# Spectral mixing and gated FFN: splitting the spectrum straight from its bank, mixing in two steps, and three smaller edits

## The chip, the cores and the metric

The kernel runs on one core of one Trainium2 chip. The metric is device time in microseconds (us), the median of several runs. Five engines work side by side, each through its own queue of instructions in order: PE (TensorE, matmuls; PEld is its weight load), DVE (VectorE), ACT (ScalarE), POOL (GpSimd) and SP (SyncE, which here only issues DMAs). An instruction whose inputs aren't ready holds up everything behind it on its engine.

## What is computed

```python
def _attn_ref(x, w_r, w_i, b_r, b_i):           # x: 8 x 3008 x 256
    X = np.fft.rfft(x, axis=1)
    Xr, Xi = X.real, X.imag
    Yr = Xr @ w_r - Xi @ w_i + b_r
    Yi = Xr @ w_i + Xi @ w_r + b_i
    Yr = np.sign(Yr) * np.maximum(np.abs(Yr) - 0.01, 0.0)   # Yi likewise
    return np.fft.irfft(Yr + 1j * Yi, n=x.shape[1], axis=1)

def _moe_ref(x, w_gate, w_val, w_out):          # x: 24064 x 256, hidden 1536
    g = x @ w_gate
    return (g / (1 + np.exp(-g)) * (x @ w_val)) @ w_out
```

A Fourier transform along the sequence, a complex 256x256 mix of the channels, a soft threshold, the inverse transform, and then a gated feed-forward network over all 24064 tokens.

## The kernel before, in words

**Two parts.** `transform` does the spectral part for 8 batches; `gated_ffn` does the feed-forward network for 24 blocks of tokens. The FFN's instructions are put in order by hand. In the transform a scheduler decides at build time in which order each engine runs its instructions, from the order in which the program emits them and from what depends on what.

**The transform.** The length 3008 is factored as 47 x 64. For each batch:

- `stage_a` (16 chunks `ch`): a load of the tokens, one fp32 matmul by the 47-point matrix into bank `ps_a` (L295, two hardware matmuls in the trace), a copy to SBUF by ACT (L298), and a store to a DRAM buffer `d1` (L299). Batch 0 goes first and alone: its loads (L286) are issued at once, its matmuls use four banks in turn, and its copies go to the tile tags "a", "z", "t" in turn, two buffers each.
- `stage_b` (12 pairs `p` of frequencies): a load `a_in` (L306), four fp32 matmuls into the one bank `ps_b` (L311), a copy `f` by ACT (L315), the sum of real and imaginary part by POOL (L316), and the split of all three (real, imaginary, sum: 768 columns) into two parts for the mix: `f_hi`, rounded to float32r (L318, DVE), and `f_lo`, what is left over (L319, DVE). `f`, `f_hi` and `f_lo` have two buffers each.
- `stage_mix`: six matmuls of the sum with one weight into bank `ps_s` (L329), an add of the bias by DVE that spreads the result over a bank `mixb0` or `mixb1` (L331), twelve matmuls onto that bank (L337), four copies that regroup it into `t` (L349, ACT), the soft threshold (L350 on DVE, L351 on POOL) and the split of the result into `y_hi` (L354, ACT) and `y_lo` (L355, DVE).
- `stage_bi`: three matmuls into `ps_z` (L368; six for a batch's first pair, L365), a copy `z` (L370, ACT) and a store to a buffer `d2` (L371).
- `stage_ai` (8 units): a load `z_in` (L379), matmuls into two banks `ps_x` (L388), copies `xt` (L395, ACT) and a store to `xt_d` (L396), from which the FFN reads its tokens.

All of this is emitted slot by slot: 96 slots, one for each (batch, pair). In slot `s` stand `stage_bi` of pair s-2, `stage_mix` of pair s-1 and `stage_b` of pair s; the `stage_a` and `stage_ai` of other batches and the preparation of the FFN's weights (L213 to L257: DVE, POOL and ACT) are spread over the slots by a few rates. Slots from 98 on are emitted by `finish`.

**The FFN's start.** `load_x(0)` loads the first block's tokens; `x_sum` makes four sums of it (L502, POOL); `x_part` splits seven operands into a float32r part (L510, ACT) and what is left (L511, POOL). The first matmul of the FFN is L745; L516 is the helper through which all its products go, three matmuls each. The first pass over a unit of weights uses the operands in the order 1, 5, 6, 2, 7, 3, 4.

Of the kernel before, what the change touches and what calls it, by code (L numbers as in the profile page):

```python
# [18 lines left out]
B = 8  # L19
# [94 lines left out]
def f32(ap):  # L114
    return ap.bitcast(F32)
# [30 lines left out]
def transform(ctx, tc, front, last, ps_, xp, w_r, w_i, cb, wup_raw, wdn_raw, ca, cf, ci, co, wdn, wup_d, xt_d, d2):  # L146
# [143 lines left out]
    def stage_a(b, ch, xt):  # L290
        if ch == 0:
            d1[b] = dram.tile([NK, P, C], F32, name="d1", tag="d1")
        tag = "absz"[ch % 4] if b == 0 else "a"
        ps = ps_.tile([P, T], F32, name="ps_a", tag="ps_" + tag)
        nc.tensor.matmul(ps[:96], lhsT=wa, rhs=xt, start=True, stop=True)  # L295
        tag = "azt"[ch % 3] if b == 0 else "a"
        a = sb.tile([96, T], F32, name="a", tag=tag)
        nc.scalar.copy(a, ps[:96])  # L298
        store = nc.sync.dma_start(d1[b].rearrange("k (q m) c -> (k q) (m c)", m=NM)[:, ch * T : (ch + 1) * T], a)  # L299
        if b == 0 and ch == NCH - 1:  # L300
            gates.append(store)


    def stage_b(b, p):
# [3 lines left out]
        for cc in range(2):  # L308
            for k in range(2):
                s = (cc * 2 + k) * P  # L310
                nc.tensor.matmul(ps[:, s : s + P], lhsT=t[:, k, cc * P : (cc + 1) * P], rhs=wf[:, 2 * p + k, :], start=True, stop=True)  # L311
        f = sb.tile([P, 3 * C], F32, name="f", tag="f", bufs=2)
        hi = sb.tile([P, 3, 2, P], F32R, name="f_hi", tag="f_hi")
        lo = sb.tile([P, 3, 2, P], F32R, name="f_lo", tag="f_lo")
        nc.scalar.copy(f[:, : 2 * C].rearrange("p (q a b) -> p a q b", q=2, b=64), ps.rearrange("p (a q b) -> p a q b", q=2, b=64))  # L315
        nc.gpsimd.tensor_tensor(f[:, 2 * C :], f[:, :C], f[:, C : 2 * C], op=ALU.add)  # L316
        flat = lambda x: x.rearrange("p q a b -> p (q a b)")
        v.tensor_copy(flat(hi), f)  # L318
        v.tensor_tensor(flat(lo), f, f32(flat(hi)), op=ALU.subtract)  # L319
        return hi, lo  # L320

    def stage_mix(b, p, parts):

# [3 lines left out]
        for cc in range(2):  # L327
# [83 lines left out]
    for b in range(B):  # L411
        base = NP * b
        for p in range(NP):
            s = base + p
            at(s, lambda b=b, p=p: fs.__setitem__((b, p), stage_b(b, p)))
            at(s + 1, lambda b=b, p=p: ys.__setitem__((b, p), stage_mix(b, p, fs.pop((b, p)))))
            at(s + 2, lambda b=b, p=p: stage_bi(b, p, ys.pop((b, p))))
    for k in range((B - 1) * NCH):
# [28 lines left out]
    for s in sorted(slots):  # L447
        if s < B * NP + 2:
            for fn in slots[s]:
                fn()  # L450
        gates += stores
        stores.clear()

    def finish():
        for s in sorted(slots):
            if s >= B * NP + 2:
                for fn in slots[s]:
                    fn()
# [4 lines left out]
def gated_ffn(ctx, tc, front, ring, ps_, co, wdn, wup_d, xt_d, d2, out):  # L463
# [35 lines left out]

    def x_sum(blk, o, a, b):  # L500
        f = lambda i: raws[blk][:, i, :]
        g.tensor_tensor(f(o), f(a), f(b), op=ALU.subtract)  # L502

    SUMS = ((4, 0, 1), (6, 2, 4), (5, 2, 0), (7, 3, 6))

    def x_part(blk, n_):
        h = BLOCKS[blk][1]
        src = raws[blk][:, X_AT[n_], :]
        part = xs[blk][n_] = sb.tile([P, 2, T], F32R, name="x_parts", bufs=12)
        act.copy(part[:, 0, :h], src)  # L510
        g.tensor_tensor(part[:, 1, :h], src, f32(part[:, 0, :h]), op=ALU.subtract)  # L511

# [306 lines left out]
```

## Time and profile before

| | us |
|---|---|
| median of 3 runs | 2745.8 (2737.93 to 2747.36) |
| the profiled execution's own time | 2740.56 |
| its span in the profile | 2738.8 |
| PE busy in the span | 2655.4 |
| DVE, POOL, ACT busy | 2087.3, 2061.7, 1712.2 |
| first matmul of the FFN starts | 679.88 |

The granted TensorE clock of the profiled execution is 0.991 of full speed on the mean. A row of the timeline gives start, duration, engine, line, operation, output and input, the count of merged instructions, and in square brackets the idle time before it and what ended that. Ends of matmuls are modelled, so a busy PE isn't PE at its peak.

### The profile page before, as it was taken

To read this page: it belongs to the slowest core of one execution; us is meant where nothing else is said; L and a number is where in the kernel's file an instruction comes from. 1 tells how busy PE (TensorE), PEld (TensorE's weight loads), DVE (VectorE), ACT (ScalarE), POOL (GpSimd) and SP (SyncE) were. 2 spreads that over 40 slices of the span, in tenths; PEclk is the share of its full clock that TensorE was granted. 3 is DMA by queue.
4 is the path that set the end of the run, shared out by engine and by line. 5 is a ranking of instruction groups with operands and counts; after the bars stand their busy time and mean duration, and the time that the engine had idled before them with its cause. 6 is when DMAs were issued, how large, how long until landed. Compare 5 with 4: busy or idle time off the path is not lost. (4 is left out here: it accounts for less than half of the span.)

```text
span 2738.8 us, 39634 instructions
## 1 busy us (share of the span) xinstructions
PE 2655.4 (97%) x13173; PEld 2207.0 (81%) x13173; DVE 2087.3 (76%) x2916; ACT 1712.2 (63%) x3280; POOL 2061.7 (75%) x1574
## 2 busy tenths in 40 slices
PE   8989998989999999999999999999999999999998
PEld 5777787778788888888888888888888888888898
DVE  3776677775778777887787877787778877888787
ACT  4666666666566666666666666666665666666665
POOL 1454465564888888888888888888888888888885
PEclk9999999999999999999999999999999999999999
DMA  8889898766354444444454444444454444444453
GB/s 251 256 271 294 283 293 267 229 197 203 137 172 156 156 141 164 168 155 157 140 171 161 150 156 149 170 156 157 140 172 156 162 144 146 154 164 153 146 185 105
DMA packets 180124, 491.88 MB, mean 180 GB/s; under 512 B 17264, under 2 KB 89584, under 8 KB 179824
## 3 DMA queue, kind: packets, MB, share of 16 engines
q1 hardware_dynamic: 179920, 489.35, 54.0%
q8 instruction: 105, 1.72, 0.3%
q14 instruction: 99, 0.81, 0.1%
HBM read 378.65 MB, written 110.62 MB: 179 GB/s over the span
## 5 line engine op out<-in xcount | busy, mean ns | idle before, releaser
L516 PE MATMUL bank<-x_parts,wup 128*128 128x512 f32 (+1 forms) x6048 | 1518.2, 386 | 1.2 <-POOL x_parts L511 0.7
L516 PEld LDWEIGHTS bank<-x_parts,wup 128*128 128x128 f32 x6048 | 1125.8, 188 | 226.5 <-DVE bank L645 5.4
L536 POOL TENSOR_TENSOR h_parts<-more,h_parts 128x512 fp32r<-128x512 f32 (+1 forms) x573 | 847.6, 1492 | 113.9 <-ACT h_parts L532 99.8
L536 POOL TENSOR_TENSOR h_parts<-hidden,h_parts 128x512 fp32r<-128x512 f32 (+1 forms) x432 | 565.1, 1316 | 204.0 <-ACT h_parts L532 164.5
L516 PE MATMUL bank<-h_parts,wdn_hi 128*128 128x512 f32 (+1 forms) x2016 | 613.5, 385 | 0.9 <-POOL h_parts L536 0.9
L532 ACT CAST h_parts<-hidden 128x512 fp32r<-128x512 f32 (+1 forms) x432 | 265.0, 613 | 451.3 <-DVE hidden L618 451.3
L516 PEld LDWEIGHTS bank<-h_parts,wdn_hi 128*128 128x128 f32 x2016 | 378.2, 188 | 74.1 <-POOL h_parts L536 1.8
L618 DVE TENSOR_TENSOR hidden<-hidden,bank 128x512 f32<-128x512 f32 (+1 forms) x576 | 376.0, 674 | 77.6 <-PE bank L516 69.2
L557 DVE TENSOR_TENSOR sums<-sums,bank 128x512 f32<-128x512 f32 (+1 forms) x360 | 241.9, 672 | 245.1 <-PE bank L516 245.1
L516 PE MATMUL bank<-h_parts,wdn_lo 128*128 128x512 f32 (+1 forms) x1008 | 388.6, 386 | 4.2 <-DVE sums L557 4.2
L532 ACT CAST h_parts<-more 128x512 fp32r<-128x512 f32 (+1 forms) x576 | 351.4, 610 | 41.8 <-DVE more L527 31.3
L616 ACT ACTIVATE hidden<-bank 128x512 f32<-128x512 f32 (+1 forms) x432 | 252.2, 584 | 117.6 <-PE bank L516 117.2
L527 DVE TENSOR_TENSOR more<-hidden 128x512 f32<-128x512 f32 (+1 forms) x288 | 293.0, 1056 | 0.0
L527 DVE TENSOR_TENSOR more<-hidden,more 128x512 f32<-128x512 f32 (+1 forms) x288 | 258.6, 898 | 0.0
L351 POOL TENSOR_TENSOR t<-t,y 128x512 f32<-128x512 f32 x96 | 133.4, 1389 | 136.6 <-DVE y L350 136.6
L645 DVE TENSOR_TENSOR bank<-hidden,bank 128x512 f32<-128x512 f32 (+1 forms) x288 | 197.0, 684 | 45.0 <-PE bank L516 32.2
L623 ACT COPY bank<-bank 128x512 f32<-128x512 f32 (+1 forms) x288 | 161.6, 561 | 109.4 <-DVE hidden L618 104.0
L516 PEld LDWEIGHTS bank<-h_parts,wdn_lo 128*128 128x128 f32 x1008 | 189.5, 188 | 40.8 <-issue 4.5
L511 POOL TENSOR_TENSOR x_parts<-xf,x_parts 128x512 fp32r<-128x512 f32 (+1 forms) x168 | 209.9, 1268 | 11.5 <-PE bank L516 7.1
L316 POOL TENSOR_TENSOR f<-f 128x256 f32<-128x256 f32 x96 | 85.3, 889 | 146.0 <-ACT f L315 142.9
L631 ACT COPY hidden<-bank 128x512 f32<-128x512 f32 (+1 forms) x288 | 167.6, 582 | 2.6
L349 ACT COPY t<-mixb 64x256 f32<-64x256 f32 x384 | 140.6, 366 | 29.6 <-PE mixb L337 20.1
(94 smaller groups left out, 3273.3 us busy)
## 6 DMA issues: line engine op xcount, KB each, us to landing
wup<-wup_d SPq DMA_DIRECT2D x288, 896.0 KB, 4.6
d<-a SPq DMA_DIRECT2D x128, 192.0 KB, 4.2
a_in<-d SPq DMA_DIRECT2D x96, 256.0 KB, 4.5
out<-o SPq DMA_DIRECT2D x88, 256.0 KB, 6.1
scratch<-xp SPq DMA_DIRECT2D x116, 192.0 KB, 4.6
d<-z SPq DMA_DIRECT2D x84, 256.0 KB, 3.8
z_in<-d SPq DMA_DIRECT2D x56, 384.0 KB, 5.1
xt_d<-xt SPq DMA_DIRECT2D x56, 376.0 KB, 4.4
```

Of the source, the lines that this page charges most:

```text
L349: nc.scalar.copy(t[64 * half : 64 * half + 64, k * C : (k + 1) * C], mixb[64 * k : 64 * k + 64, half * C : (half + 1) * C])
L511: g.tensor_tensor(part[:, 1, :h], src, f32(part[:, 0, :h]), op=ALU.subtract)
L516: nc.tensor.matmul(o, lhsT=weights[w], rhs=parts[x], start=start and i == 0, stop=stop and i == 2, skip_group_check=True)
L527: v.tensor_tensor(at(o, h), at(a, h), at(b, h), op=ALU.subtract)
L532: act.copy(pair[i][:, 0, :h], at(i, h))
L536: eng.tensor_tensor(pair[i][:, 1, :h], at(i, h), f32(pair[i][:, 0, :h]), op=ALU.subtract)
L557: v.tensor_tensor(o, o, spare[:, :h], op=ALU.add)
L616: act.activation(at(i, h), src, AF.Silu)
L618: v.tensor_tensor(at(i, h), at(i, h), src, op=ALU.mult)
L623: act.copy(b3[:, :h], b1[:, :h])
L631: act.copy(m5, b2[:, :h])
L645: v.tensor_tensor(b2[:, :h], m5, b3[:, :h], op=ALU.add)
```

## The change

Four edits.

1. **Batch 0's copies** go in turn to six tags instead of three, "a", "z", "t", "y", "y_hi", "y_lo": twelve buffers instead of six.
2. **The split in `stage_b`** is taken from the bank `ps_b` itself. ACT writes `f_hi` of the real and the imaginary part from the bank (512 columns, L320 of the changed kernel) and copies the real part to `f` (256 columns, L321). DVE adds the imaginary part from the bank (L322) and takes `f_lo` of both parts, bank minus `f_hi` (L323). The sum's own split is ACT's for the upper part (L324) and DVE's for the lower (L325). POOL has no work left here. `f_hi` and `f_lo` get three buffers each; `f` is a third of its size.
3. **The mix in two steps.** The six matmuls and the bias add become `stage_sum`, one slot after `stage_b`; the rest stays `stage_mix`, one slot later; `stage_bi` comes one slot later than it did. `finish` begins at slot 99.
4. **The FFN's first block.** The split of operand 1 is emitted ahead of the sums; the four sums go to DVE; of the seven lower parts those of operands 6, 7 and 4 go to DVE, and 1, 5, 2 and 3 stay on POOL. Later blocks are as before.

```diff
-        tag = "azt"[ch % 3] if b == 0 else "a"
+        tag = ("a", "z", "t", "y", "y_hi", "y_lo")[ch % 6] if b == 0 else "a"
         a = sb.tile([96, T], F32, name="a", tag=tag)
...
-        f = sb.tile([P, 3 * C], F32, name="f", tag="f", bufs=2)
-        hi = sb.tile([P, 3, 2, P], F32R, name="f_hi", tag="f_hi")
-        lo = sb.tile([P, 3, 2, P], F32R, name="f_lo", tag="f_lo")
-        nc.scalar.copy(f[:, : 2 * C].rearrange("p (q a b) -> p a q b", q=2, b=64), ps.rearrange("p (a q b) -> p a q b", q=2, b=64))
-        nc.gpsimd.tensor_tensor(f[:, 2 * C :], f[:, :C], f[:, C : 2 * C], op=ALU.add)
-        flat = lambda x: x.rearrange("p q a b -> p (q a b)")
-        v.tensor_copy(flat(hi), f)
-        v.tensor_tensor(flat(lo), f, f32(flat(hi)), op=ALU.subtract)
+        total = sb.tile([P, 2 * P], F32, name="f", tag="f", bufs=2)
+        hi = sb.tile([P, 3, 2, P], F32R, name="f_hi", tag="f_hi", bufs=3)
+        lo = sb.tile([P, 3, 2, P], F32R, name="f_lo", tag="f_lo", bufs=3)
+        both = ps.rearrange("p (a q b) -> p a q b", q=2, b=64)
+        first = lambda x: x[:, :2].rearrange("p q c (k b) -> p (c k) q b", b=64)
+        blocks = lambda x: x.rearrange("p (a b) -> p a b", b=64)
+        flat = lambda x: x[:, 2].rearrange("p c a -> p (c a)")
+        nc.scalar.copy(first(hi), both)
+        nc.scalar.copy(blocks(total), both[:, :, 0])
+        v.tensor_tensor(blocks(total), blocks(total), both[:, :, 1], op=ALU.add)
+        v.tensor_tensor(first(lo), both, f32(first(hi)), op=ALU.subtract)
+        nc.scalar.copy(flat(hi), total)
+        v.tensor_tensor(flat(lo), total, f32(flat(hi)), op=ALU.subtract)
         return hi, lo
 
-    def stage_mix(b, p, parts):
+    def stage_sum(b, p, parts):
...
+        return parts
+
+    def stage_mix(b, p, parts):
+
+        mixb = mixed[p % 2]
         for half, (q, i) in enumerate(((1, 2), (0, 1))):
...
-            at(s + 1, lambda b=b, p=p: ys.__setitem__((b, p), stage_mix(b, p, fs.pop((b, p)))))
-            at(s + 2, lambda b=b, p=p: stage_bi(b, p, ys.pop((b, p))))
+            at(s + 1, lambda b=b, p=p: fs.__setitem__((b, p), stage_sum(b, p, fs.pop((b, p)))))
+            at(s + 2, lambda b=b, p=p: ys.__setitem__((b, p), stage_mix(b, p, fs.pop((b, p)))))
+            at(s + 3, lambda b=b, p=p: stage_bi(b, p, ys.pop((b, p))))
...
-    for sums_ in SUMS:
-        x_sum(0, *sums_)
-    for n_ in X_AT:
-        x_part(0, n_)
+    x_part(0, 1)
+    for sums_ in SUMS:
+        x_sum(0, *sums_, eng=v)
+    for n_ in list(X_AT)[1:]:
+        x_part(0, n_, v if n_ in (6, 7, 4) else g)
```

**What moves on the engines.** The rows below are the built program's order on one engine; a name with a number, like ps_x_7095 or mixb_120, is one buffer or bank of that name.

ACT, one of the last slots of the transform, before:

```order
L349 COPY t<-mixb_120 64x256 x4
L315 COPY f<-ps_b 128x4x2x64
L395 COPY xt<-ps_x_7095 128x376
L395 COPY xt<-ps_x_7101 128x376
L370 COPY z<-ps_z 128x512
L354 CAST y_hi<-t 128x512
```

The same place in the changed program (L360 is the old L349, L406 the old L395, L381 the old L370, L365 the old L354):

```order
L320 CAST f_hi<-ps_b 128x4x2x64
L321 COPY f<-ps_b 128x256
L360 COPY t<-mixb_120 64x256 x4
L324 CAST f_hi<-f 128x256
L406 COPY xt<-ps_x_7268 128x376
L381 COPY z<-ps_z 128x512
L406 COPY xt<-ps_x_7274 128x376
L365 CAST y_hi<-t 128x512
```

One ACT instruction on a pair's spectrum has become three, and the four copies of `t` now stand between the second and the third.

DVE, one slot near the end of the transform, before:

```order
L318 CAST f_hi<-f 128x768
L355 TENSOR_TENSOR y_lo<-t,y_hi 128x512
L319 TENSOR_TENSOR f_lo<-f,f_hi 128x768
L331 TENSOR_TENSOR mixb_121<-ps_s,bias 128x512
L350 TENSOR_SCALAR y<-t 128x512
```

The same engine in the changed program (L366 is the old L355, L337 the old L331, L361 the old L350):

```order
L366 TENSOR_TENSOR y_lo<-t,y_hi 128x512
L322 TENSOR_TENSOR f<-f,ps_b 128x256
L323 TENSOR_TENSOR f_lo<-ps_b,f_hi 128x4x2x64
L337 TENSOR_TENSOR mixb_121<-ps_s,bias 128x512
L361 TENSOR_SCALAR y<-t 128x512
L325 TENSOR_TENSOR f_lo<-f,f_hi 128x256
```

The two wide instructions of the split have become three narrower ones, two of which read the bank.

PE, the end of the transform and the FFN's first matmul, before (here the number behind a name is one tile; ps_z_7276 is the last pair's):

```order
L337 MATMUL mixb1_121<-wm1_lo_116,f_hi_7171 128x256
L368 MATMUL ps_z_7209<-y_hi_7159,wi_hi_111 128x512
L368 MATMUL ps_z_7209<-y_lo_7160,wi_hi_111 128x512
L368 MATMUL ps_z_7209<-y_hi_7159,wi_lo_112 128x512
L368 MATMUL ps_z_7276<-y_hi_7244,wi_hi_111 128x512
L368 MATMUL ps_z_7276<-y_lo_7245,wi_hi_111 128x512
L368 MATMUL ps_z_7276<-y_hi_7244,wi_lo_112 128x512
L745 MATMUL bank_7293<-x_parts_7314,wdn_hi_60 128x512
```

The same place in the changed program (L348 is the old L337, L379 the old L368, L399 the old L388, L759 the old L745; ps_z_7468 is the last pair's):

```order
L348 MATMUL mixb1_121<-wm1_lo_116,f_hi_7330 128x256
L379 MATMUL ps_z_7437<-y_hi_7397,wi_hi_111 128x512
L399 MATMUL ps_x0_7424<-wo_956,z_in_7368 128x94 x4
L379 MATMUL ps_z_7437<-y_lo_7398,wi_hi_111 128x512
L379 MATMUL ps_z_7437<-y_hi_7397,wi_lo_112 128x512
L399 MATMUL ps_x1_7430<-wo_956,z_in_7368 128x94 x4
L379 MATMUL ps_z_7468<-y_hi_7464,wi_hi_111 128x512
L379 MATMUL ps_z_7468<-y_lo_7465,wi_hi_111 128x512
L379 MATMUL ps_z_7468<-y_hi_7464,wi_lo_112 128x512
L759 MATMUL bank_7485<-x_parts_7502,wdn_hi_60 128x512
```

Eight matmuls of the last `stage_ai` have moved from earlier on PE to between the last mix and the last `ps_z`.

More of the change, by code (lines that the diff above doesn't have):

```diff
@@ L447, in transform @@
     for s in sorted(slots):
-        if s < B * NP + 2:
+        if s < B * NP + 3:
             for fn in slots[s]:
@@ L455, in finish @@
         for s in sorted(slots):
-            if s >= B * NP + 2:
+            if s >= B * NP + 3:
                 for fn in slots[s]:
@@ L498, in load_x, with x_sum, x_part @@
         xs[blk] = {}
-    def x_sum(blk, o, a, b):
+    def x_sum(blk, o, a, b, eng=g):
         f = lambda i: raws[blk][:, i, :]
-        g.tensor_tensor(f(o), f(a), f(b), op=ALU.subtract)
+        eng.tensor_tensor(f(o), f(a), f(b), op=ALU.subtract)
     SUMS = ((4, 0, 1), (6, 2, 4), (5, 2, 0), (7, 3, 6))
-    def x_part(blk, n_):
+    def x_part(blk, n_, eng=g):
         h = BLOCKS[blk][1]
@@ L510, in x_part @@
         act.copy(part[:, 0, :h], src)
-        g.tensor_tensor(part[:, 1, :h], src, f32(part[:, 0, :h]), op=ALU.subtract)
+        eng.tensor_tensor(part[:, 1, :h], src, f32(part[:, 0, :h]), op=ALU.subtract)
     def product(o, weights, parts, start, stop):
```

## The prediction

> **What bounds the kernel now.** I read the windows of the whole span first: each engine's busy time, then the granted TensorE clock and the DMA share.
>
> ```profile
> 0.00:40.00 40.00, 27.10 (x65) 12.98 (x65) 6.08 (x11) 14.30 (x25) 1.45 (x6) 0.87 0.86 244
> 40.00:240.00 200.00, 184.68 (x1164) 148.44 (x1164) 136.49 (x195) 131.12 (x284) 99.21 (x92) 0.98 0.84 265
> 240.00:440.00 200.00, 183.93 (x1223) 153.05 (x1222) 145.10 (x198) 130.26 (x285) 109.26 (x99) 0.98 0.88 291
> 440.00:640.00 200.00, 177.73 (x1256) 155.55 (x1255) 148.66 (x201) 127.52 (x282) 118.29 (x102) 0.98 0.73 228
> 640.00:680.00 40.00, 35.72 (x273) 33.03 (x271) 18.72 (x31) 27.94 (x63) 11.46 (x12) 0.96 0.55 179
> 690.00:2738.80 2048.80, 2037.14 (x9176) 1698.69 (x9174) 1630.91 (x2281) 1274.80 (x2331) 1713.41 (x1258) 1.00 0.46 155
> ```
>
> From 690 us on PE is busy 2037.14 of 2048.80 us: the FFN is bound by PE, and the change leaves it alone but for its first block. All that can move lies ahead of 690. From 40 to 640 PE is busy 184.68 + 183.93 + 177.73 = 546.3 of 600 us and idle 53.7; in the first 40 us it is idle 12.9. No other engine is full there: DVE 430.2, ACT 388.9, POOL 326.8 of 600. So the transform is bound by PE plus the waits of PE, and the waits of PE between 40 and 640 us tell what a change of the other engines can be worth:
>
> ```profile
> PE mixb L337 <- DVE mixb L331: 18.7, 22, 2.1
> PE ps_x L388 <- DMA z_in<-d: 9.4, 10, 2.1
> PE ps_z L368 <- DVE y_lo L355: 8.7, 9, 3.0
> PE ps_a L295 <- ACT a L298: 6.0, 7, 3.1
> PE ps_z L368 <- ACT y_hi L354: 4.1, 5, 1.6
> PE ps_z L368 <- ACT z L370: 3.7, 4, 2.2
> ```
>
> The columns are us in total, times, and the longest. The largest is the bias add L331 coming late; y_lo and y_hi (12.8) end the soft threshold's chain over ACT, DVE and POOL.
>
> **Edit 1, twelve buffers.** Batch 0's matmuls on PE, and the copy on ACT that held them up:
>
> ```profile
> 18.83 2.52 ACT L298 COPY a<-ps_a 96x512 f32<-96x512 f32 x5 [4.77 <-DMA d<-a]
> 9.76 7.11 PE L295 MATMUL ps_a<-x_first,wa 96*96 96x512 f32 x16 [0.82 <-DMA x_first<-xp]
> 19.46 5.37 PE L295 MATMUL ps_a<-x_first,wa 96*96 96x512 f32 x8 [2.59 <-ACT a L298]
> 24.67 1.88 PE L295 MATMUL ps_a<-scratch,wa 96*96 96x512 f32 x4
> 15.00:20.00 5.00, 2.41 (x7) 0.76 (x6) 0.00 (x0) 1.17 (x3) 0.00 (x0) 1.00 0.95 312
> 20.00:25.00 5.00, 5.00 (x9) 1.74 (x8) 0.00 (x0) 2.65 (x6) 0.00 (x0) 0.66 0.80 259
> 25.00:30.00 5.00, 1.55 (x4) 0.33 (x2) 0.00 (x0) 1.61 (x3) 0.00 (x0) 1.00 0.67 200
> ```
>
> The seventh copy waited 4.77 us for the first store to land; PE stood 2.59 us and then ran its next eight matmuls at 0.67 us each instead of 7.11 / 16 = 0.44, the granted clock at 0.66. With twelve buffers copies 7 to 12 need no store, and the first store has landed before the thirteenth. The last twelve matmuls would take 12 x 0.44 = 5.3 us from 16.87, ending at 22.2 instead of 26.55: 4.4 us. But the DMA engines were idle only 0.05 + 0.20 + 0.33 of 5 us each there, 2.9 us, and the same bytes must pass. Bounds 1 (earlier stores delay the last loads) and 4.4; I take **3.5**.
>
> The Trainium skill, "TensorE: Matmul & The Clock Gate", section "What's actually happening", has the clock halve only after an idle window of about 3.4 us; here the granted clock is down after a gap of 2.59 us. By that page the drop needn't go with the gap, and this edit would give the gap alone, 2.6, and the sum below would be 0.9 smaller.
>
> **Edits 2 and 3, the steady slots.** The groups of the split and the mix, 40 to 640 us:
>
> ```profile
> L315 ACT COPY f<-ps_b 128x512 f32<-128x512 f32 x92 | 54.0, 587 | 59.0 <-DVE f_lo L319 51.2 <-PE ps_b L311 4.0 <-PE ps_x L388 1.6
> L316 POOL TENSOR_TENSOR f<-f 128x256 f32<-128x256 f32 x92 | 82.4, 896 | 103.0 <-ACT f L315 99.9 <-DVE y L350 3.0
> L318 DVE CAST f_hi<-f 128x768 fp32r<-128x768 f32 x90 | 73.1, 813 | 46.4 <-PE mixb L337 43.7 <-POOL f L316 2.7
> L319 DVE TENSOR_TENSOR f_lo<-f,f_hi 128x768 fp32r<-128x768 f32 x91 | 102.7, 1128 | 1.4
> L331 DVE TENSOR_TENSOR mixb<-ps_s,bias 128x512 f32<-128x512 f32 x90 | 62.1, 690 | 0.5 <-PE ps_s L329 0.5
> L349 ACT COPY t<-mixb 64x256 f32<-64x256 f32 x356 | 130.4, 366 | 27.7 <-PE mixb L337 18.5 <-ACT z L370 2.0 <-issue 2.0
> L354 ACT CAST y_hi<-t 128x512 fp32r<-128x512 f32 x88 | 54.6, 620 | 57.4 <-POOL t L351 56.9
> ```
>
> The new widths by the nearest rows:
>
> ```profile
> 34.10 0.40 ACT L210 CAST wi_hi<-raw_i 128x256 fp32r<-128x256 f32 x1 [2.89 <-DMA raw_i<-ci]
> 34.54 0.42 DVE L211 TENSOR_TENSOR wi_lo<-raw_i,wi_hi 128x256 fp32r<-128x256 f32 x1 [0.21 <-ACT wi_hi L210]
> ```
>
> ACT loses 0.587 a pair and gains a 512-wide cast from the bank (between L315's 0.587 and L354's 0.620; I take 0.60), a 256-wide copy (L349, 0.37) and a 256-wide cast (L210, 0.40): +0.78, over 96 pairs 75 us. DVE loses 0.813 + 1.128 = 1.94 and gains a 256-wide add (L211, 0.42), a 512-wide subtract with one operand in a bank (L331's shape, 0.69) and a 256-wide subtract (0.42 alone; 0.50 with L319's surplus, 1.128 on the mean against 0.95 in the slot below): 1.61, so -0.33, 32 us. POOL loses 0.896 a pair, 86 us.
>
> What this does to PE's waits. L331 stands behind L318 and L319 in DVE's queue, and L318 itself waited 43.7 us for PE: `f_hi` had two buffers, so each write stood, with L331 behind it, until the mix two pairs back had read them. One slot of the trace:
>
> ```profile
> 645.97 0.56 DVE L318 CAST f_hi<-f 128x768 fp32r<-128x768 f32 x1 [2.45 <-PE mixb L337]
> 647.05 0.95 DVE L319 TENSOR_TENSOR f_lo<-f,f_hi 128x768 fp32r<-128x768 f32 x1
> 647.92 0.69 DVE L331 TENSOR_TENSOR mixb<-ps_s,bias 128x512 f32<-128x512 f32 x1
> ```
>
> After the change ACT writes `f_hi`, with three buffers, and what can stand ahead of L331 is shorter. Of the 18.7 us I take 14 as gone (none, if the new DVE work is as late as the old; all 18.7 at best). Of the threshold's 12.8 us I take 5: the 0.9 us on POOL and the 0.33 on DVE that could stand in its way, over 4 to 5 of its 14 waits. On ACT the 51.2 us that L315 waited for L319, everything behind it waiting too, go, and 75 us of work come: 24 us more of 600. PE's waits on ACT's copies a and z (9.7) may grow; I charge **3**. New is that `ps_b` is held longer: one copy of 0.59 before, now the cast, the copy, the add and the subtract, 0.60 + 0.37 + 0.42 + 0.69 = 2.08 plus handovers. PE returns to `ps_b` once in a slot of 600 / 92 = 6.5 us, so the other five matmul groups cover it; if that cover goes, a slot pays up to 1.5 us. Sum of the steady slots: 14 + 5 - 3 = **16**, bounds 8 (half) and 24 (all of L331, 8 of the threshold, 3 saved on a and z). The waits for z_in are DMA's and stay.
>
> A slot more of depth costs nothing while other groups fill it; at the start DMA is the limit anyway (share 0.86). I charge 0, at worst 3.
>
> **The transform's end.** PE's last matmuls:
>
> ```profile
> 676.74 0.80 PE L368 MATMUL ps_z<-y_hi,wi_hi 128*128 128x512 f32 x1 [2.87 <-ACT y_hi L354]
> 679.88 0.80 PE L745 MATMUL bank<-x_parts,wdn_hi 128*128 128x512 f32 x1 [1.19 <-ACT x_parts L510]
> 651.89 1.87 PEld L388 LDWEIGHTS ps_x<-wo,z_in 96*128 96x128 f32 x16
> ```
>
> PE idles 2.87 us for the last threshold. The order now puts eight matmuls of `stage_ai` there, sixteen weight loads, 1.87 us: **1.9** gained, 0 to 1.9.
>
> **Edit 4, the FFN's first block.**
>
> ```profile
> 679.20 3.74 ACT L510 CAST x_parts<-xf 128x512 fp32r<-128x512 f32 x7
> 679.90 8.72 POOL L511 TENSOR_TENSOR x_parts<-xf,x_parts 128x512 fp32r<-128x512 f32 x7 [3.87 <-ACT x_parts L510]
> 688.68 3.57 PE L516 MATMUL bank<-x_parts,wup 128*128 128x512 f32 x13 [0.28 <-POOL x_parts L511]
> 622.43 5.20 POOL L502 TENSOR_TENSOR xf<-xf 128x512 f32<-128x512 f32 x3 [0.69 <-PE ps_z L365]
> ```
>
> PE's first pass waits for POOL: seven lower parts of 1.25 us, the last at 688.6. With four on POOL those end at 679.9 + 4 x 1.25 = 684.9; DVE's three (0.69 each) follow the casts, which end at 682.9, so by 683.7. PE can start the seventh product near 685.7 instead of 688.68: **3.0**, bounds 2 and 3.7 (688.6 - 684.9). The four sums, 6.5 us on POOL around 622 to 631, become about 4 x 0.69 = 2.8 us on DVE, off PE's path: 0.
>
> **Sum.** 3.5 + 16 + 1.9 + 3.0 = 24.4 us off the profiled execution's 2740.6: 2716.2. The median is 5.2 us above that execution, so I forecast **2721**; by the bounds 11 to 34 us, 2712 to 2735.
>
> **The rivals.** *A, slower: ACT becomes the limit.* ACT runs in order, and the new cast of the sum waits for DVE's add, with the regrouping copies or `z` behind it. It decides from the point where ACT's work and waits in a slot exceed PE's 6.5 us; ACT had 388.9 / 92 = 4.2 busy and gets 5.0. If every third slot then pays the added 0.78, 25 us are lost, and none of the 16 is gained: 25 - 8.4 = 17 more, 2762. Against it: only 9.7 of PE's waits end on those copies. The Trainium skill, "ScalarE: Activation LUTs", section "Rules for kernel authors", advises VectorE over ScalarE for adds, multiplies and the like; by that advice the new copies stand on the wrong engine, and the trace has them cheaper on neither (0.40 and 0.42 at 256 columns).
>
> *B, no change: the two steps were there already.*
>
> ```profile
> 658.29 0.28 PE L329 MATMUL ps_s<-wm_lo,f_hi 128*128 128x256 f32 x1
> 661.71 0.37 PE L337 MATMUL mixb<-wm_hi,f_hi 128*128 128x256 f32 x1
> ```
>
> Between a sum and its mix the scheduler already put 3.4 us of other matmuls, so the emitted slots may alter little; if DVE's new pieces come as late as the old, only 3.5 + 1.9 + 3.0 = 8.4 remain: 2737.
>
> *C, more: contention goes with POOL's work.* DVE's L319 takes 1.128 on the mean and 0.95 where POOL rests, while L331, which reads a bank, takes 0.690 in both. POOL loses a quarter of its 326.8 us, and L322 and L323 read the bank. If all of PE's waits on the bias add and the threshold go (18.7 + 12.8) with the 8.4, that is 40 us: 2706. Against it: the new cast of the sum needs DVE again.
>
> The Trainium skill, "SBUF — State Buffer", section "Who interferes with whom", gives the rule behind C: a DVE instruction with two SBUF inputs contends with GpSimd's reads, one with a single SBUF input does not. The two rows agree.
>
> **How the numbers follow.** Chances: forecast 0.48, A 0.12, B 0.26, C 0.14. About 0.5%, 13.7 us, is what a measurement of this kernel can tell from no change. The forecast's bounds reach 3 us into that band, so of its 0.48 some 0.04 falls there, and of B 0.02 beyond its other end. Faster: 0.44 + 0.14 = 0.58; within: 0.24 + 0.04 = 0.28; slower: 0.12 + 0.02 = 0.14. The range leaves out most of A and the far side of C: 2698 to 2752.
>
> **What would show it.** In the changed profile: no wait of L298 for d<-a before 25 us, and PE's batch 0 matmuls without the 2.59 us gap; PE's wait for the bias add under 5 us; PE idle from 40 to 640 us down from 53.7 to about 38; the FFN's seventh product about 6 us after its first matmul instead of 688.68 - 679.88 = 8.8. It is wrong if ACT passes 80% busy in those windows with PE waiting on L321 or L323 for `ps_b`, or if the wait on the bias add stays.

## The result, and the profile after

The changed kernel took 2698.84 us (median of 4 runs, 2696.98 to 2702.40) against 2744.99 us for the kernel before beside it: ratio 0.9846 [0.9830, 0.9862], 42 us by the ratio (46 by the two medians). The profiled execution took 2697.08 us with a span of 2695.3, against 2740.56 and 2738.8. The forecast was 2721 with a range of 2698 to 2752: right in direction, and the gain is 1.7 times the 24.4 us that the sum gave. The measured time lies 0.8 us inside the range, whose lower end was put there for rival C and not for the sum. That the range holds it is luck; the sum missed by 18 us.

The windows of the changed kernel, in the columns of the prediction's first fence (PE, PEld, DVE, ACT, POOL busy with counts, granted TensorE clock, DMA share, GB/s):

```profile
0.00:40.00 40.00, 27.60 (x74) 14.56 (x75) 7.76 (x16) 16.53 (x30) 0.73 (x5) 0.83 0.94 274
40.00:240.00 200.00, 189.87 (x1238) 154.73 (x1237) 130.98 (x243) 157.22 (x368) 71.57 (x62) 1.00 0.86 277
240.00:440.00 200.00, 188.09 (x1270) 157.96 (x1270) 129.98 (x238) 153.20 (x361) 80.31 (x72) 0.99 0.92 300
440.00:640.00 200.00, 191.58 (x1402) 172.11 (x1401) 133.06 (x241) 160.79 (x379) 82.64 (x72) 0.99 0.75 238
690.00:2695.30 2005.30, 1993.96 (x8991) 1665.22 (x8989) 1599.44 (x2238) 1248.65 (x2284) 1680.79 (x1234) 1.00 0.45 155
```

From 40 to 640 us PE is busy 189.87 + 188.09 + 191.58 = 569.5 us, 23 more than before, in the same 600 us; ACT 471.2 (388.9 before), DVE 394.0 (430.2), POOL 234.5 (326.8). The granted clock is 1.00, 0.99, 0.99 where it was 0.98 three times. The FFN starts earlier and then takes as long as it did: its first matmul stands at 637.34 instead of 679.88, 42.5 earlier, and from there to the end of the span are 2058.0 us now and 2058.9 before. So all of the gain but about 1 us is made before the FFN.

What PE waits for, in the changed kernel from 40 to 600 us (us in total, times, longest; 600 lies about as far ahead of the FFN's first matmul as 640 did before):

```profile
PE ps_x L399 <- DMA z_in<-d: 11.3, 12, 2.2
PE ps_z L379 <- DVE y_lo L366: 3.1, 6, 1.1
PE mixb L348 <- DVE mixb L337: 3.0, 2, 2.6
PE ps_b L311 <- DVE f_lo L323: 2.4, 4, 1.3
PE ps_a L295 <- ACT a L298: 1.9, 4, 0.8
```

The bias add (now L337) went from 18.7 to 3.0 us. The threshold's y_lo and y_hi, 12.8 together, are 3.1; the copies a and z, 9.7 together, are 1.9, and z no longer appears. New is the wait for `ps_b`, 2.4, and the transfers z_in rose from 9.4 to 11.3. The small waits that aren't in these rows rose too, from 2.3 us in all to 5.0. The largest wait left is a DMA's.

The start, in PE's timeline and two windows of the changed kernel:

```profile
9.07 10.54 PE L295 MATMUL ps_a<-x_first,wa 96*96 96x512 f32 x24 [0.65 <-DMA x_first<-xp]
19.45 1.88 PE L295 MATMUL ps_a<-scratch,wa 96*96 96x512 f32 x4
31.12 2.08 PE L311 MATMUL ps_b<-wf,a_in 128*128 128x128 f32 x8 [3.16 <-DMA a_in<-d]
15.00:20.00 5.00, 5.00 (x13) 1.91 (x12) 0.00 (x0) 3.34 (x7) 0.00 (x0) 1.00 1.04 355
20.00:25.00 5.00, 1.33 (x4) 0.21 (x2) 0.00 (x0) 1.40 (x3) 0.00 (x0) 0.84 1.03 383
```

All 24 matmuls of batch 0 run without a gap at 10.54 / 24 = 0.44 us, and the four behind them end at 21.33 instead of 26.55. The DMA engines are now full from 15 to 25 us (1.04 and 1.03, before 0.95 and 0.80). PE then stands again, the last time for `a_in`, and the first pair's matmul comes at 31.12 instead of 34.97: 3.9 us. The granted clock falls while PE stands there: it is 0.50 from 25 to 35 us, where it was 1.00 and 0.63 in the two halves of that stretch before.

The groups of the split, the bias add and the threshold's last step, 40 to 640 us (out<-in, count | busy us, mean ns | idle before, what ended it):

```profile
L366 DVE TENSOR_TENSOR y_lo<-t,y_hi 128x512 fp32r<-128x512 f32 x96 | 74.5, 776 | 64.7 <-ACT y_hi L365 64.2
L337 DVE TENSOR_TENSOR mixb<-ps_s,bias 128x512 f32<-128x512 f32 x96 | 66.4, 692 | 15.2 <-PE ps_s L335 14.8
L323 DVE TENSOR_TENSOR f_lo<-ps_b,f_hi 128x512 fp32r<-128x512 f32 x94 | 64.2, 683 | 0.0
L320 ACT CAST f_hi<-ps_b 128x512 fp32r<-128x512 f32 x94 | 55.2, 587 | 10.1 <-PE ps_b L311 8.9
L325 DVE TENSOR_TENSOR f_lo<-f,f_hi 128x256 fp32r<-128x256 f32 x94 | 50.3, 536 | 7.5 <-ACT f_hi L324 6.9
L322 DVE TENSOR_TENSOR f<-f,ps_b 128x256 f32<-128x256 f32 x94 | 39.3, 418 | 48.9 <-ACT f L321 48.2
L324 ACT CAST f_hi<-f 128x256 fp32r<-128x256 f32 x94 | 38.5, 410 | 20.9 <-DVE f L322 20.1
L321 ACT COPY f<-ps_b 128x256 f32<-128x256 f32 x94 | 35.8, 381 | 0.0
```

Before, ACT waited 51.2 us for DVE's `f_lo`, POOL 99.9 for ACT, and DVE 43.7 for PE. Now ACT waits 20.1 for DVE's sum, DVE waits 48.2 for ACT's copy, and DVE no longer stands for PE's mix. Before, the bias add stood ready behind DVE's other work (0.5 us of idle ahead of it); now DVE waits 14.8 us for PE's sum. The late one has changed sides.

Where the 42.5 us are, by PE's window from 40 us to the FFN's first matmul, of before:

```profile
40.00:680.00 640.00, 582.05 (x3909) 490.06 (x3908) 448.96 (x623) 416.84 (x914) 338.21 (x304) 0.98 0.80 256
```

and of the changed kernel:

```profile
40.00:637.50 597.50, 567.03 (x3901) 483.30 (x3899) 392.57 (x718) 468.70 (x1100) 232.01 (x205) 0.99 0.85 272
```

PE was idle 640 - 582.05 = 58.0 us before and 30.5 now, 27.5 less. The other 15.0 are busy time. The 8 records fewer (3909 before, 3901 now) are worth about 1 us of that. More than half of the rest is the clock. The 0.98 of before is no steady clock: from 40 to 676 us it is 1.00 but for five stretches at 0.50, four of 3.4 us and one of 6.8, near 106, 216, 284, 509 and 577 us. This is the first of them, with the window ahead of it (before):

```profile
102.99:106.40 3.41, 0.47 (x2) 0.42 (x3) 1.55 (x4) 0.60 (x2) 0.72 (x1) 1.00 0.95 330
106.40:109.81 3.41, 3.41 (x13) 2.41 (x11) 3.41 (x7) 1.69 (x3) 1.82 (x2) 0.50 0.49 172
```

PE was busy 19.8 us in these five; the changed kernel has one such stretch from 40 to 634 us, with 3.4 us. At half the clock that makes (19.8 - 3.4) / 2, about 8 us of shorter matmuls. Some 6 us of busy time are not accounted for. Fewer waits may be part of it: matmuls of the mix that follow each other start 0.12 us apart and last 0.28, and one behind a wait has nothing to overlap with. That is argued, not shown.

### The profile page after: what moved, and what is told of

Same layout as the page of the kernel before. It is cut to its first block, busy times and chain, and to the rows that moved or that the text cites. A ratio compares the mean times of both kernels' runs of the same rounds, so it can differ in the third digit from the quotient of the medians.

```text
span 2695.3 us, 39771 instructions
## 1 busy us (share of the span) xinstructions
PE 2640.1 (98%) x13173; PEld 2203.1 (82%) x13173; DVE 2037.1 (76%) x3019; ACT 1766.4 (66%) x3472; POOL 1953.1 (72%) x1471
## 5 line engine op out<-in xcount | busy, mean ns | idle before, releaser
L548 POOL TENSOR_TENSOR h_parts<-more,h_parts 128x512 fp32r<-128x512 f32 (+1 forms) x573 | 848.2, 1493 | 113.2 <-ACT h_parts L544 99.9
L657 DVE TENSOR_TENSOR bank<-hidden,bank 128x512 f32<-128x512 f32 (+1 forms) x288 | 196.9, 684 | 36.1 <-PE bank L528 24.1
L360 ACT COPY t<-mixb 64x256 f32<-64x256 f32 x384 | 140.7, 366 | 13.3 <-PE mixb L348 9.4
L399 PEld LDWEIGHTS ps_x<-wo,z_in 96*128 96x128 f32 x896 | 116.5, 191 | 31.8 <-DMA z_in<-d 13.9
```

The costliest lines, as they stand in the source:

```text
L360: nc.scalar.copy(t[64 * half : 64 * half + 64, k * C : (k + 1) * C], mixb[64 * k : 64 * k + 64, half * C : (half + 1) * C])
L548: eng.tensor_tensor(pair[i][:, 1, :h], at(i, h), f32(pair[i][:, 0, :h]), op=ALU.subtract)
L657: v.tensor_tensor(b2[:, :h], m5, b3[:, :h], op=ALU.add)
```

## The experiments

The theory taken from the prediction was that the split, with a third buffer, frees the bias add on DVE. The rivals were that the two steps of the mix do it, that POOL's work out of the way does it, or the shorter DVE queue. Ratios are to the kernel before, run on the same chip. An added operation writes a tile that nothing reads; its line shifts the later lines by one or two.

**One part at a time.** Edit 1 alone:

```diff
-        tag = "azt"[ch % 3] if b == 0 else "a"
+        tag = ("a", "z", "t", "y", "y_hi", "y_lo")[ch % 6] if b == 0 else "a"
```

> The kernel before with edit 1 alone (twelve buffers for batch 0). In the changed kernel the first stage_b matmul stood at 31.12 us instead of 34.97. If that head start is carried to the end: 3.9 us faster, 2741 us. Rival, that the slots after it are paced by DMA (its share there is 0.94 in the first 40 us) and the head start is given back by the first mixes: within 1 us of before, 2744 to 2745 us.

Ratio 0.9988 [0.9980, 0.9997], 3.3 us faster (0.8 to 5.5). PE's row of the first pair in its timeline:

```profile
31.23 2.08 PE L311 MATMUL ps_b<-wf,a_in 128*128 128x128 f32 x8 [3.45 <-DMA a_in<-d]
```

It stands where it stands in the changed kernel: this edit makes the whole gain at the start. That isn't the chance of one execution, though the start varies: in the seven kernels here with the old copies the first pair comes at 31.90 to 37.52 us (35.0 on the mean), in the seven with the new at 30.58 to 31.50 (31.2).

Edit 2 alone, the split with its third buffer, the mix still in one slot:

```diff
-        nc.scalar.copy(f[:, : 2 * C]..., ps...)
-        nc.gpsimd.tensor_tensor(f[:, 2 * C :], f[:, :C], f[:, C : 2 * C], op=ALU.add)
-        v.tensor_copy(flat(hi), f)
-        v.tensor_tensor(flat(lo), f, f32(flat(hi)), op=ALU.subtract)
+        (the new six operations; f_hi, f_lo with bufs=3)
```

> The kernel before with edit 2 alone (split from the bank, f_hi and f_lo with three buffers; mix in one slot). Theory of the prediction, that the steady slots gain by the split's move between engines and the third buffer: nearly all of the 37 us of the steady slots, 2706 to 2713 us, PE's wait for the bias add (L331) under 5 us. Rival, that the two emitted steps carry it: 2730 us or more, and the wait for the bias add still over 12 us.

2712.46 us, ratio 0.9887 [0.9874, 0.9900]: 31 us faster, three quarters of the whole. Its waits of PE, 40 to 640 us:

```profile
PE ps_x L393 <- DMA z_in<-d: 11.3, 11, 1.8
PE mixb L342 <- DVE mixb L336: 5.5, 4, 2.9
PE ps_b L311 <- DVE f_lo L322: 4.0, 4, 2.3
```

The time is the theory's, and the bias add's wait falls to 5.5 without the two steps, close to the 5 that was expected.

Edit 3 alone, the mix in two steps:

```diff
-    def stage_mix(b, p, parts):
+    def stage_sum(b, p, parts):
...
+    def stage_mix(b, p, parts):
...
-            at(s + 1, ... stage_mix ...)
-            at(s + 2, ... stage_bi ...)
+            at(s + 1, ... stage_sum ...)
+            at(s + 2, ... stage_mix ...)
+            at(s + 3, ... stage_bi ...)
```

> The kernel before with edit 3 alone (the sum and the mix in two slots, still two buffers of f_hi and f_lo). Theory of the prediction: the scheduler already had 3.4 us of other matmuls between a sum and its mix, so within 6 us of before, 2739 to 2751 us. Rival, that the steps carry the gain: 15 us or more faster, 2730 us or less.

Ratio 1.0025 [1.0015, 1.0035]: 6.9 us slower. Its waits, 40 to 640 us:

```profile
DVE f_hi L318 <- PE mixb L342: 58.2, 37, 3.5
PE mixb L342 <- DVE mixb L331: 23.9, 25, 3.0
```

`f_hi` is now held a slot longer with two buffers, so DVE stands 58.2 us for PE (43.7 before), and the wait on the bias add grows too. The two steps do not carry the gain; alone they cost slightly more than the 6 us allowed for.

Edit 4 alone, the FFN's first block on two engines:

```diff
+    x_part(0, 1)
     for sums_ in SUMS:
-        x_sum(0, *sums_)
-    for n_ in X_AT:
-        x_part(0, n_)
+        x_sum(0, *sums_, eng=v)
+    for n_ in list(X_AT)[1:]:
+        x_part(0, n_, v if n_ in (6, 7, 4) else g)
```

> The kernel before with edit 4 alone (first block's operands on POOL and DVE). The prediction's term was 3.0 us: 2742 us. From the changed kernel's profile, where four parts on POOL take 6.36 us (1.59 each, 1.25 before) and three on DVE take 0.84 and 2 x 1.60, and the first hidden part's product comes 15.79 us after the FFN's first matmul instead of 16.50: 0.7 us, 2744 us. Rival, that the sums on DVE disturb the last slots: 2 us or more slower, 2747 us.

Ratio 0.9997 [0.9987, 1.0007]: no difference that can be told from none. From the FFN's first matmul to the first product of the hidden layer its trace has 15.81 us, 0.7 less than before.

**Which half of the split it is.** Only a third buffer for `f_hi` and `f_lo`, the old split kept:

```diff
-        hi = sb.tile([P, 3, 2, P], F32R, name="f_hi", tag="f_hi")
-        lo = sb.tile([P, 3, 2, P], F32R, name="f_lo", tag="f_lo")
+        hi = sb.tile([P, 3, 2, P], F32R, name="f_hi", tag="f_hi", bufs=3)
+        lo = sb.tile([P, 3, 2, P], F32R, name="f_lo", tag="f_lo", bufs=3)
```

> The kernel before with a third buffer for f_hi and f_lo and nothing else. Theory, that the buffer was what held L331 (L318 stood 43.7 us for PE, L331 behind it): that wait under 15 us, PE's wait for the bias add under 8 us, 10 to 16 us faster, 2726 to 2732 us. Rival, that the work's move from POOL and DVE to ACT is what counts: within 5 us of before, 2737 us or more.

Ratio 0.9990 [0.9981, 1.0000], 2.7 us. Its waits, 40 to 640 us:

```profile
DVE f_hi L318 <- POOL f L316: 24.3, 17, 3.7
PE mixb L337 <- DVE mixb L331: 17.7, 21, 2.3
DVE f_hi L318 <- PE mixb L337: 9.0, 9, 1.9
```

DVE's stand for PE falls from 43.7 to 9.0 as meant, and PE's wait for the bias add stays (17.7 of 18.7): DVE now waits for POOL's sum (24.3; 2.7 before). The time is the rival's. DVE's whole stand ahead of `f_hi` fell only from 46.4 to 33.3 us, so the stand for PE was not by itself what made the bias add late: with the old split POOL's sum is late next.

The new split with two buffers, the mix in one slot (edit 2 as above, but `bufs=2`):

```diff
+        hi = sb.tile([P, 3, 2, P], F32R, name="f_hi", tag="f_hi", bufs=2)
+        lo = sb.tile([P, 3, 2, P], F32R, name="f_lo", tag="f_lo", bufs=2)
```

> The kernel before with edit 2 but two buffers of f_hi and f_lo, mix in one slot. Theory, now that the third buffer alone gave 3 us and the split in two steps with two buffers was slower than before: the third buffer is what the second step needs, and the split in one slot gains without it, 20 us or more faster, 2722 us or less. Rival, that the split needs it in any case, since ACT's write of f_hi then stands for PE's mix with all of ACT's queue behind it: 2735 us or more.

2752.62 us, ratio 1.0047 [1.0028, 1.0066]: 13 us slower, not 20 faster, so the rival's time came. Its waits, 40 to 640 us:

```profile
DVE mixb L336 <- PE ps_s L334: 66.4, 37, 6.2
PE ps_x L393 <- DMA z_in<-d: 21.3, 15, 3.2
PE ps_a L295 <- DMA scratch<-xp: 15.4, 13, 4.1
PE mixb L342 <- DVE mixb L336: 15.0, 17, 2.7
```

The same operations as in the 31 us gain, one buffer fewer, and PE waits 10 us more for z_in, 15.4 for `scratch` and 9.5 more for the bias add. DVE was mostly not the late one: it waited 66.4 us for PE's sum. The old split had a copy `f` of its own, in two buffers, between the bank and `f_hi`; without it the bank is emptied only when `f_hi` is free, two mixes back. That this is the path is argued from the code and not shown. The sign of it would be ACT standing for the mix at `f_hi`; in this trace ACT waits 7.3 us there, all for `ps_b`, and its 38.5 us of waiting for the mix are at the copies `t`. The build puts the engines' work in another order for each variant, so a wait may have moved ahead of its place, but that wasn't tested.

The whole change with two buffers:

```diff
-        hi = sb.tile([P, 3, 2, P], F32R, name="f_hi", tag="f_hi", bufs=3)
-        lo = sb.tile([P, 3, 2, P], F32R, name="f_lo", tag="f_lo", bufs=3)
+        hi = sb.tile([P, 3, 2, P], F32R, name="f_hi", tag="f_hi", bufs=2)
+        lo = sb.tile([P, 3, 2, P], F32R, name="f_lo", tag="f_lo", bufs=2)
```

> The changed kernel with two buffers of f_hi and f_lo instead of three. Theory, that the third buffer carries the gain: 12 us or more above the changed kernel, 2708 us or more, and ACT's write of f_hi (L320) waiting for PE's mix by 30 us or more. Rival, that the move between engines carries it: within 5 us of the changed kernel, 2695 to 2701 us.

2755.13 us, ratio 1.0043 [1.0028, 1.0058]: 54 us above the changed kernel for one buffer of each tile. The theory's size came, and its sign did not: ACT's write L320 waits 8.8 us, all for `ps_b`, none for the mix. Its middle window:

```profile
240.00:440.00 200.00, 180.79 (x1124) 149.44 (x1124) 111.96 (x205) 136.05 (x316) 67.21 (x62) 0.92 0.81 261
```

Every engine does less in the 200 us, and the granted clock is 0.92.

The two steps with the third buffer, the old split:

```diff
+        hi = sb.tile([P, 3, 2, P], F32R, name="f_hi", tag="f_hi", bufs=3)
+        lo = sb.tile([P, 3, 2, P], F32R, name="f_lo", tag="f_lo", bufs=3)
...
+            at(s + 1, ... stage_sum ...)
+            at(s + 2, ... stage_mix ...)
+            at(s + 3, ... stage_bi ...)
```

> The kernel before with edit 3 and a third buffer of f_hi and f_lo, the split as before. Theory, that two steps with three buffers are worth some us by themselves, as they were on top of the split (the whole change gains 42 us, the edits alone 31, 3 and 1): 2732 to 2737 us. Rival, that they help only once DVE's queue is short: 2738 us or more, as with the third buffer alone.

Ratio 0.9994 [0.9984, 1.0003]: no difference, as the rival had it. Its waits of PE, 40 to 640 us:

```profile
PE ps_z L373 <- DVE y_lo L360: 13.2, 18, 1.4
PE mixb L342 <- DVE mixb L331: 11.3, 9, 4.1
```

The bias add's wait did fall, from 18.7 to 11.3, and y_lo's rose from 8.7 to 13.2. With the sum a slot ahead of the mix, the same late DVE is waited for at another place.

The eight kernels together, us against before, worked out from the ratios:

| `f_hi`, `f_lo` | old split | new split | old split, two steps | new split, two steps, edits 1 and 4 |
|---|---|---|---|---|
| two buffers | 0 | +13 | +7 | +12 |
| three buffers | -3 | -31 | -2 | -42 |

Neither the new split nor the third buffer gains much alone (+13 and -3, and -31 together). The two steps gain about 7 us where both are there: 42 less 31, 3.3 and 0.8. The four intervals together leave about 7 us of uncertainty on that, so it is hardly told from none.

**What in the new split.** Each of the next three gives back to the changed kernel one of the things that the split took away, or takes more of what it costs. First POOL, an add of 256 columns a pair (`f` in three buffers, so that nobody waits for it):

```diff
+    spare = k1p.tile([P, 2 * P], F32, name="spare")
...
-        total = sb.tile([P, 2 * P], F32, name="f", tag="f", bufs=2)
+        total = sb.tile([P, 2 * P], F32, name="f", tag="f", bufs=3)
...
         nc.scalar.copy(flat(hi), total)
+        nc.gpsimd.tensor_tensor(spare, total, total, op=ALU.add)
```

> The changed kernel with one more POOL add of 128x256 a pair, which nothing reads: 0.9 us a pair, about the work that POOL had lost. Rival C of the prediction, that DVE gains because POOL no longer contends with it: 8 us or more above the changed kernel, 2704 us or more, with y_lo (776 ns) and the weight preparation on DVE longer again. Theory, that contention is a small part: within 4 us, 2693 to 2700 us.

2705.98 us, ratio 0.9873 [0.9854, 0.9891]: some 7 us above the changed kernel (0.0027, with about 0.0024 of uncertainty either way), between the two expectations. Its groups, 40 to 640 us:

```profile
L368 DVE TENSOR_TENSOR y_lo<-t,y_hi 128x512 fp32r<-128x512 f32 x95 | 81.4, 857 | 54.0 <-ACT y_hi L367 53.6
L326 POOL TENSOR_TENSOR spare<-f 128x256 f32<-128x256 f32 x94 | 65.6, 698 | 87.3 <-DVE f L323 85.5 <-DMA scratch<-xp 1.5
L324 DVE TENSOR_TENSOR f_lo<-ps_b,f_hi 128x512 fp32r<-128x512 f32 x94 | 64.2, 683 | 0.0
```

With POOL's add back, y_lo takes 857 ns again (776 without it, 844 before), while L324, with one operand in a bank, stays at 683. So contention is there. The add is 65.6 us of the 82.4 that POOL had lost, and it costs about a quarter of what the split gained, with room from nearly nothing to a half. It does not bring back all of the contention: the weight preparation's L227 (L228 here) took 928 ns before, 737 in the changed kernel and 759 here. And PE's waits stay short with it: from 40 to 600 us 4.1 on y_lo and y_hi, 3.9 on the bias add.

Then ACT, one more copy of 256 columns a pair:

```diff
+    spare = k1p.tile([P, 2 * P], F32, name="spare")
...
         nc.scalar.copy(flat(hi), total)
+        nc.scalar.copy(spare, total)
```

> The changed kernel with one more ACT copy of 128x256 a pair, which nothing reads: 0.38 us a pair, 36 us in all. Rival A of the prediction, that ACT is at its limit (it is 77 to 80% busy): 12 us or more above the changed kernel (a third of it), 2708 us or more. Theory, that ACT still has room: within 4 us, 2693 to 2700 us.

Ratio 0.9856 [0.9842, 0.9871], 3 us above the changed kernel, within the uncertainty. Its first window:

```profile
40.00:240.00 200.00, 189.33 (x1219) 155.91 (x1219) 127.64 (x241) 164.22 (x396) 69.08 (x62) 0.97 0.85 275
```

ACT is at 82% here, 83% in the two windows behind, and the kernel hardly notices, though PE waits 6.1 us for `ps_b` on the added copy: the 12 us of rival A lie outside the uncertainty (about 6 us), so ACT isn't the limit.

Then DVE, an add of 256 columns a pair with one operand in a bank, so that POOL isn't in it, behind the bias add:

```diff
+    spare = k1p.tile([P, C], F32, name="spare")
...
+        v.tensor_tensor(spare, p1[:, :C], bias[0][:, 0, :], op=ALU.add)
         return parts
```

> The changed kernel with one more DVE add of 128x256 a pair, right behind the bias add, which nothing reads; one operand is in a bank, so that by its shape (0.42 us) it adds to DVE's queue and little to contention: 40 us of DVE's work, about what the split and the lesser contention took from it (4.06 us a pair before, 3.57 now). Theory, that the steady slots gain because DVE's queue is shorter: 12 us or more above the changed kernel, 2711 us or more, PE's wait for the bias add over 8 us. Rival, that it is POOL's work and the hand-overs that count: within 4 us, 2695 to 2703 us.

2706.46 us, ratio 0.9884 [0.9866, 0.9901]: 8 to 10 us above the changed kernel, with some 6 us of uncertainty. (Its profiled execution took 2714.31, the other three 2705 to 2706.) The group of the added operation, 40 to 640 us:

```profile
L341 DVE TENSOR_TENSOR spare<-ps_s,bias 128x256 f32<-128x256 f32 x95 | 39.2, 413 | 0.0
```

and PE's wait for the bias add in the same stretch:

```profile
PE mixb L350 <- DVE mixb L338: 2.2, 2, 1.3
```

39.2 us more on DVE cost a quarter of that, less than the 12 us that the theory wanted, and not by the wait on the bias add, which was to pass 8 and stays at 2.2. By which wait it costs is not shown; the granted clock is 1.00, 0.97 and 0.97 in the three windows, lower than the 1.00, 0.99 and 0.99 of the changed kernel.

**The FFN's first block.** All seven lower parts on DVE, none on POOL:

```diff
-    x_part(0, 1)
+    x_part(0, 1, v)
...
-        x_part(0, n_, v if n_ in (6, 7, 4) else g)
+        x_part(0, n_, v)
```

> The changed kernel with all seven lower parts of the FFN's first block on DVE. Theory, that POOL and DVE slow each other there (POOL 1.59 us a part instead of 1.25, DVE 1.60 instead of 0.69): seven parts in about 7 x 0.69 = 4.9 us, all ready 1.4 us earlier than now, the first hidden product 1 to 2 us earlier after the FFN's first matmul than 15.79; 2698 us, at the edge of what the runs tell. Rival, that another wait is next (the bank add L657 on the same engine): 15.8 us or later.

Ratio 0.9854 [0.9839, 0.9869], the same as the changed kernel. Its timeline:

```profile
638.66 4.30 DVE L523 TENSOR_TENSOR x_parts<-xf,x_parts 128x512 fp32r<-128x512 f32 x7 [1.95 <-ACT x_parts L522]
644.11 5.77 PE L528 MATMUL bank<-x_parts,wup 128*128 128x512 f32 x21 [0.17 <-DVE bank L657]
654.02 0.39 PE L528 MATMUL bank<-h_parts,wdn_lo 128*128 128x512 f32 x1
```

Seven parts on DVE alone take 4.30 us, less than the same seven on two engines. The first product of the hidden layer comes 15.34 us after the first matmul of the FFN (654.02 - 638.68), against 15.79 in the changed kernel: less than the 1 to 2 us expected, since PE's next group still waits for the bank add L657, as the rival had it in part.

## Why the prediction was right or wrong

**Edit 1, 3.5 us: right.** 3.9 in the trace and 3.3 by the edit alone. Batch 0's gap and its slow matmuls went together, as the row-based bound had it, and the DMA engines, now full, took back part: batch 0's last matmuls end 5.2 us earlier (21.33 against 26.55), the first pair starts 3.9 earlier. The Trainium skill, "TensorE: Matmul & The Clock Gate", section "What's actually happening", has the clock halve after an idle window of about 3.4 us, so that by it the slow matmuls would have stayed and the edit given 2.6. The measurement differs: with the gap of 2.59 us gone, no matmul of batch 0 is slow any more, so there the clock's drop did go with the gap. It came back behind it, though, where PE now waits for `a_in` (0.50 from 25 to 35 us), and the first mix starts at 40.91 instead of 43.00, so that in the changed kernel 2.1 of the 3.9 us are left there.

**The prices of the operations: right.** ACT was to gain 0.78 us a pair and gains 0.587 + 0.381 + 0.410 - 0.587 = 0.79. DVE's three new ones were put at 1.61 and take 0.418 + 0.683 + 0.536 = 1.64.

**The steady slots, 16 us: mis-sized; about 37 measured** (42.5 less 3.9 for the start and 1.2 for the end). That lies above the upper bound too. The bound was added up wrongly: all of L331, 8 of the threshold and 3 saved make 18.7 + 8 + 3 = 29.7, not 24. By its terms:

- *The bias add, 14 of 18.7.* It is 15.7, so the size was right. The reason was not: "each write stood, with L331 behind it, until the mix two pairs back had read them" is not borne out by the third buffer alone, which took most of that stand away (43.7 to 9.0) and left 17.7 of the wait, with POOL's late sum in its place. It takes the split and the buffer together.
- *The threshold, 5 of 12.8.* It is 9.7 (12.8 less 3.1). "over 4 to 5 of its 14 waits" was the step that failed; nearly all of them got shorter. y_lo itself is shorter with less of POOL beside it (776 ns for 844), but that isn't why: with POOL's add back it takes 857, and the waits on y_lo and y_hi are still 4.1. The split with its third buffer brings them down alone (2.9 in edit 2's run, from 40 to 600 us). That y_lo starts sooner, in a DVE queue with less in it, is argued.
- *The charge of 3 for a and z.* It is a gain of 7.8. The prediction weighed 51.2 us of ACT's wait that would go against 75 us of work that would come. The row that bore on it is the wait: an engine that stands holds up all that is behind it, and one that is busy 52 us longer over the same slots (468.7 against 416.8 from 40 us to the FFN's first matmul) but waits less can serve PE earlier. That the shorter wait is the reason is argued. The copy added to ACT shows that still more work on it costs little here.
- *`ps_b` held longer.* The price was "a slot pays up to 1.5 us" if cover fails. It fails 4 times for 2.4 us in all: right at nearly nothing.
- *The clock.* No term for it was in the sum. Where PE's waits closed, four of the five stretches at half the clock went with them, about 8 us by the accounting above, nearly a quarter of the 37. In the whole change with two buffers it went the other way, to 0.92 in one window.

Together 15.7 + 9.7 + 7.8, less 2.4 for `ps_b`, 1.9 for z_in and a balance of 1.4 in small waits and the end of the transform, is 27.5 of idle time. With the clock's 8 it comes to about 36.

**A slot more of depth, 0: right only with the third buffer.** The two steps alone cost 6.9 us, which the bound of 3 didn't reach; with the third buffer and the old split they cost about 1 (-2 against -3).

**The transform's end, 1.9 us: right in kind, 1.2 in the trace.** The moved matmuls fill the hole before the last threshold:

```profile
634.20 0.64 PE L379 MATMUL ps_z<-y_hi,wi_hi 128*128 128x512 f32 x1 [1.65 <-ACT y_hi L365]
```

PE's wait there is 1.65 instead of 2.87, with 16 records of `stage_ai` moved in ahead of it. This part was not run alone.

**The FFN's first block, 3.0 us: wrong, 0.7.** The changed kernel's timeline:

```profile
637.34 0.80 PE L759 MATMUL bank<-x_parts,wdn_hi 128*128 128x512 f32 x1 [1.19 <-ACT x_parts L522]
637.37 6.36 POOL L523 TENSOR_TENSOR x_parts<-xf,x_parts 128x512 fp32r<-128x512 f32 x4 [3.87 <-ACT x_parts L522]
639.40 3.19 DVE L523 TENSOR_TENSOR x_parts<-xf,x_parts 128x512 fp32r<-128x512 f32 x2 [0.20 <-ACT x_parts L522]
642.51 0.68 DVE L657 TENSOR_TENSOR bank<-hidden,bank 128x512 f32<-128x512 f32 x1
643.25 5.75 PE L528 MATMUL bank<-x_parts,wup 128*128 128x512 f32 x21 [0.53 <-DVE bank L657]
653.13 0.39 PE L528 MATMUL bank<-h_parts,wdn_lo 128*128 128x512 f32 x1
```

Two steps failed. "DVE's three (0.69 each)" beside POOL's "1.25 us" took each engine's price alone: side by side DVE's last two need 3.19 / 2 = 1.60 each (its first took 0.84) and POOL 6.36 / 4 = 1.59 a part, so POOL's four end at 643.7, 6.4 us after the first matmul, and not at 5. The Trainium skill, "SBUF — State Buffer", section "Who interferes with whom", which the prediction used for rival C, says of just this pair that it contends; the rows agree, and the prediction didn't apply it to its own term. And DVE has the bank add L657 behind its parts: it starts at 642.51 with no idle ahead of it, and PE's next group waits for it. "Near 685.7" for the seventh product, 5.8 us after the first matmul, became about 8: at 643.25, 5.9 us after it, PE had done 12 matmuls, four products, where before 20 were done at 8.8.

**The rivals.** *A, ACT the limit:* ACT was at 79% and PE waited 2.4 us on L323; with 36 us more on ACT still 3 us. It fell, though the sign that the prediction named for it came by the letter: ACT was busy 160.79 of 200 us, 80.4%, in the third window, with PE waiting on L323 for `ps_b`. *B, the two steps were there already:* true of the steps by themselves, which gain nothing with the old split (+7, -2); but DVE's new pieces do not come as late as the old, so its time was wrong. *C, contention goes with POOL's work:* nearest in time (2706), and its waits did nearly all go (31.5 to 6.1), but POOL's add put back costs only about 7 us and brings none of these waits back (4.1 and 3.9), so the mechanism is a part at most.

**What stays open.** The new split with its third buffer gained 31 us alone. Putting POOL's work back costs about 7, and 39 us of DVE's work 8 to 10; these overlap and do not add up to 31. The rest is most likely the chain itself, ACT to POOL to DVE and back to ACT's wait for DVE (51.2 us), which has one engine less now, and the clock that follows from fewer gaps. That is argued from the waits. Why the new split loses with two buffers is open too, since the wait that it was laid to is not in the traces. None of this was shown: the old split with its sum on DVE instead of POOL, and three buffers, wasn't run, and as each variant is put in another order by the build, a wait can't be swapped by itself.

## What to carry to other kernels

A copy that only stages data out of a bank is also a buffer: when it is removed, give its destination one more buffer in the same edit, or the gain can turn into a loss (here -31 us with it, +13 without). Read the waits of the engine that is waited for, not only its busy time: the one that had work added but waits taken away became the one that PE waited for less. Don't price two engines side by side on SBUF by what each takes alone, and look what is queued behind the work that you move. And count with a wait of PE what the clock does behind it: here four half-speed stretches fewer were about 8 of the 42 us.

## What the hardware showed

DVE and POOL subtracting 128x512 tiles from SBUF at the same time took 1.60 (two parts of three; the first took 0.84) and 1.59 us each, where DVE alone took 4.30 / 7 = 0.61 and POOL alone 8.72 / 7 = 1.25: together they did seven in 6.4 us, DVE alone in 4.3. An instruction of DVE with one operand in a bank took 683 ns with and without an add on POOL beside it.

A granted clock of 0.98 was full speed with a few stretches of half speed. In the kernel before, from 40 to 640 us, each of the five stretches at 0.50 came right behind a window of 3.41 us in which PE was busy for 0.47, 1.30, 0.66, 1.50 and 1.54 us; cut on from the same edges, every other window that itself had the full clock (1.83 us busy or more) was followed by the full clock. The slow matmuls of batch 0 fit it: the half-speed stretch from 21.05 us came behind 1.59 us of 3.41. The limit isn't sharp: in the changed kernel windows with 1.86 and 1.96 us busy were followed by the full clock, and one with 2.11 by half. So waits that left PE idle for more than about half of such a window cost their own length and, by estimate, up to 3.41 / 2 = 1.7 us more behind them.
